# A new order of issue for the same tasks of an attention and softplus kernel

## The chip, the core and the metric

The kernel runs on one core of a Trainium2 chip. The metric is the device time of one execution in microseconds (us); lower is better. Unless another unit stands beside it, every time below is in us. The core has TensorE (PE in the profile, with its weight loads as PEld), VectorE (DVE), ScalarE (ACT), GpSimd (POOL) and SyncE (SP), which issues the DMAs here. Each engine works through its own instructions in the order in which the program issues them, and waits where an input isn't ready.

## The reference: what is computed

A long-short attention over 4 batches, 8 heads, 768 positions and 64 columns feeds a feed-forward layer with softplus (512 to 2048 to 512 columns, 3072 tokens).

```python
k_sum = k.reshape(B, H, nb, block, D).max(axis=3)      # blocks of 32 positions
v_sum = v.reshape(B, H, nb, block, D).mean(axis=3)
scores_l = scale * np.matmul(q, k.transpose(0, 1, 3, 2))
mask_l = np.abs(pos[:, None] - pos[None, :]) < window  # window 16
scores_s = scale * np.einsum('bhsd,bhnd->bhsn', q, k_sum) + np.log(block)
scores_all = np.concatenate([np.where(mask_l, scores_l, -1e9), scores_s], axis=-1)
a = softmax(scores_all)
x = np.matmul(a, np.concatenate([v, v_sum], axis=2))   # heads side by side: 3072 x 512
h = x @ w_in                                            # 512 x 2048
g = np.maximum(h, 0.0) + np.log1p(np.exp(-np.abs(h)))
out = g @ w_out                                         # 2048 x 512
```

## The kernel before

**Attention.** The work is cut into 24 units: 12 chunks of 256 tokens (three per batch), each with two halves of the heads (called 0 and 2). A unit is named by its group x, its place i in the group and its heads: a0.0.0, a0.0.2, a0.1.0 and a0.1.2 are the units of group 0, a1.0.0 and a1.0.2 those of group 1. A unit runs through scores (PE, L601), mask (DVE, L614, eight instructions, with the row's maximum), exp (ACT, L622, eight instructions, each with the read of its sum), inverse (DVE, L629 and L630), normalise (L635, on POOL or DVE), transposes, values (PE, L692), the rounded part xh (ACT, L708) and the remainder xl (DVE, L712). The four units of group 0 are transposed by PE (L648) and copied from PSUM by ACT (L652, two copies per unit, one for each half of pT). All others are transposed by DVE in squares of 32 (L661), leave by DMA to DRAM (L669) and come back in place by four DMAs (L673). Block maxima of k are taken by DVE (L329), block sums of v by POOL or DVE (L357 to L362); of the first batch they are made by PE (L407) and scaled by ACT (L420).

**Weights.** For each of the 16 slices f of 128 hidden columns a chain w0 to w15 splits the weights of both layers into a high and a low part: two loads (SP, L741 and L738), magnitude (L754 on DVE or L757 on ACT), clamp (DVE, L761), shift (DVE, L765), sign (DVE, L769), tail (L775 on ACT or L778 on DVE), add_tail (POOL, L783), high (L787, ACT or DVE) and low (L794, DVE or POOL). All of a chain but loads, magnitude and high work in a scratch tile t, of which there are two, shared with the loads of k and v for block sums and with the output tiles. w0 and w1 are made in two halves of 128x512, all others at once as 128x1024.

**Feed-forward.** Product (PE, L823) of slice f with the tokens of group x is three matmuls for each of four slices of x: high with high, high with low, low with high. ACT applies softplus twice (L843 rounded as gh, L847 exactly), DVE takes the remainder gl (L851), and PE projects gh and gl with the second weights (L860). The work of slice f in group x is named f0.6 for x = 0, f = 6. Groups 0 and 1 are run for slices 0 to 10, then for 11 to 15, with partial sums kept in DRAM (L883 to L891); the remaining groups run over all 16.

**What sets the order.** The program first declares 1593 tasks with `order.add`, each with the buffers that it reads and writes, and with one way for each engine that could run it. It then issues them one by one as a string says:

```python
        for word in sequence.split():
            task = self.tasks[int(word.rstrip("ab"))]
            assert all(other in begun for other, _ in task.after) and task not in begun
            begun.add(task)
            task.ways[" ab".index(word[-1]) if word[-1] in "ab" else 0].run()
```

A number names a task, and the letter behind it picks another way: `198` is the low part of w4 on DVE, `198a` the same on POOL; `398` is the normalise of a1.0.0 on POOL, `398a` on DVE. So the string `SEQUENCE` (L147) fixes the order on every engine, the DMA queue of SP included, and for the tasks with two ways the engine. Waits between engines follow from the buffers that the tasks share.

Of the kernel before, what the change touches and what calls it, by code (L numbers as in the profile page):

```python
# [152 lines left out]
171a 130 109 199 94 172 40 200 110 111 173 41 112 42 174 387 175 239 113 95 197 176 121 114 123 122 115 124 198
177 219 125 220 181a 178 309 209 126 182 185 318 127 201a 183 388 310 184 240 394 202 311 210 186 319 312 408
205 313 249 203 325 187 204 320 592 390 321 188 391 225 279 314 206 322 221a 315 395 316 594 250 317 207a 323
396 208 222 331 223 224 241a 326 397 324 398a 415 399 226 327 245 329 328 400 229 332 242 230 227 330 269 243
389 333 228 337 280 215 392 244 211a 334 246 335 416 338 343 212 213 339 247 214 336 248 344 345 341 417 340 216
574 401 346 393 342 595 347 591 217a 218 348 255 578 418 575 593 419 349 402 403 231a 404 289 235 232 233 355
350 234 579 236 351 352 353 576 356 290 420 357 600a 405 237a 421 270 238 603 406 358 251a 354 407 361 577a 252
580 422 253 367 362 409 254 413 412 604 256 363 425 423 359 368 411 275 424 364 410 257a 369 360 258 605 365  # L160
581a 584 414 373 588 618 259 295 606 370 366 374 585a 371 375 582 426 589 376 299 260 372 427 428 378 377 607
429 381 382a 583 383 435 300 430 431 619 432 380 436 271 437 379 438 433 272 434 273 586 441 620 274 596 617 447
442 608 276 621 443 439 448 444 609 449 265 440 450 453 277a 305 590 278a 459 454 455 456 445 587 384 446 261
451 626a 385 452 460 262 386 461 457 598 285 263 629 264 465 643 462 266 644 630 601 471 466 648a 645 467 610
458 468 472 463 267a 473 631 474 464 291 469 470 268 477 292 483 293 478 632 294 651 475 479 633a 666 484 667
485 476 281a 296 480 481 486 634 489 635 670a 282 482 297 602 498 283 612 490 284 613 665 298 491 487 499 492
286 500 652 488 301a 506 501 287a 653 302 673 288 502 794 597 303 493 797 304 494 796 507 795 512 599 495a 306
# [15 lines left out]
1056 1048 936 1049 937 938 941 942 943 1076 946 1077 1057 1058 1059 1078 1060 952 939 947 944 1079 1080a 1081
948 945 953 950 949 1082 954 1090 955 1091 1099a 951 1061 958 1062 1069 1071 1063 1083 1084 1085 1086 964 959
1070 1072 960 1074 961 1075 970 965 1093 1092 966 1094 967 1087 956 1095 1088 1097 1089 1096 1098 1102 971 1100
972 1101 957 1103 1222 962 1226 973 1104 963 968 969 974 1105 1106a 1107 975 976 1223 1108 1227 1224 1228 982
977 1109 1110 978 1111 979 980 983 1112 984 985 988 1225a 1229a 1232 994 989 990 1236 991 1239 1240 1248 1241
1000 995 1243 996 1242 1233 981 986 997 1237 1230 1006 1001 1002 1234 1238 1231 1251 987 1252 992 1003 1253 1235
993 998 999 1007 1004 1254 1255a 1256 1008 1005 1113 1009 1257 1265 1266 1274 1010 1114 1267 1011 1014 1115 1269
1268 1012 1015 1244 1013 1017 1016 1116 1018a 1258 1259 1260 1261 1019 1245 1124 1117 1247 1118 1246 1249 1119  # L190
1250 1277 1125 1126 1120 1278 1121 1122 1127 1279 1123 1128 1262 1129 1270 1271 1263 1280 1130 1273 1281a 1272
1275 1264 1276 1282 1136 1131 1283 1292 1296 1293 1132 1291 1133 1134 1137 1138 1139 1142 1284 1285 1286 1287
1148 1143 1144 1145 1288 1149 1150 1299 1294 1289 1295 1290 1135 1297 1300 1140 1298 1151 1301 1141 1146 1147
1152 1302 1303a 1153 1304 1154 1305 1314 1318 1315 1313 1160 1155 1306 1156 1307 1157 1158 1308 1161 1309 1162
1163 1166 1310 1167 1168 1321 1316 1311 1169 1317 1312 1159 1319 1322 1164 1320 1323 1165 1170 1171 1172 1324
1325a 1326 1178 1173 1327 1174 1175 1176 1179 1180 1181 1184 1328 1329 1330 1331 1190 1185 1186 1187 1196 1191
# [815 lines left out]
```

## Time and profile before

| | |
|---|---|
| median of 3 runs | 628.37 (627.63 to 628.79) |
| profiled execution | 630.34 |
| its span in the profile | 628.5 |
| mean granted clock of TensorE | 0.992 |
| PE busy | 611.5, 97% of the span |
| DVE busy | 277.5 (44%), 757 instructions |
| ACT busy | 311.7 (50%), 752 instructions |
| POOL busy | 83.2 (13%), 74 instructions |

Rows of a timeline begin with the start and the time that the row took, then engine, line, operation and tiles, the number of instructions (a row can hold several) and, in brackets, idle time before it and what ended it. Rows of groups give the number of instructions behind the shapes, then the busy time of all and the mean of one in ns. The busy share of an engine is a mean over very different stages: the weights are prepared in the first quarter of the span only, so POOL's 13% says little of that quarter.

### The profile page before, as it was taken

To read this page: it belongs to the slowest core of one execution; us is meant where nothing else is said; L and a number is where in the kernel's file an instruction comes from. 1 tells how busy PE (TensorE), PEld (TensorE's weight loads), DVE (VectorE), ACT (ScalarE), POOL (GpSimd) and SP (SyncE) were. 2 spreads that over 40 slices of the span, in tenths; PEclk is the share of its full clock that TensorE was granted. 3 is DMA by queue.
4 is the path that set the end of the run, shared out by engine and by line. 5 is a ranking of instruction groups with operands and counts; after the bars stand their busy time and mean duration, and the time that the engine had idled before them with its cause. 6 is when DMAs were issued, how large, how long until landed. Compare 5 with 4: busy or idle time off the path is not lost.

```text
span 628.5 us, 11315 instructions
## 1 busy us (share of the span) xinstructions
PE 611.5 (97%) x4348; PEld 505.5 (80%) x4348; DVE 277.5 (44%) x757; ACT 311.7 (50%) x752; POOL 83.2 (13%) x74
## 2 busy tenths in 40 slices
PE   4889999999999999999999999999999999999997
PEld 4478888888888888888888888888888888888996
DVE  5978988679644443212451444432411111341111
ACT  1789988479652554316472435462622222553222
POOL 5324341434310202101000030000000000000000
PEclk9799999999999999999999999999999999999999
DMA  8779678933767861241344553543300400311000
GB/s 292 234 244 347 217 190 242 291 92 113 231 199 212 236 181 63 86 139 43 135 152 131 176 141 107 153 144 110 100 0 1 141 0 2 108 66 68 34 1 33
DMA packets 84453, 85.72 MB, mean 136 GB/s; under 512 B 24528, under 2 KB 70192, under 8 KB 84400
## 3 DMA queue, kind: packets, MB, share of 16 engines
q1 hardware_dynamic: 84400, 85.01, 44.0%
q8 instruction: 34, 0.56, 0.4%
q14 instruction: 19, 0.16, 0.1%
HBM read 64.23 MB, written 18.35 MB: 131 GB/s over the span
## 4 chain that ended last, share of the span: by engine, by line
PE 95%; DMA 1%; issue 1%; POOL 1%; SPq 1%; ACT 0%; DVE 0%; POOLq 0%; DVEq 0%
PE po L860 42%; PE ph L823 42%; PE sc L601 4%; PE xo L692 4%; DMA first<-v_hp_dram 1%; PE vt L407 1%; PE warm L934 1%; POOL added L296 0%; SPq L555 0%; PE pt L648 0%; DVE sp L614 0%; ACT sp L622 0%; SPq L738 0%; SPq L741 0%; ACT vn L420 0%
## 5 line engine op out<-in xcount | busy, mean ns | idle before, releaser
L823 PE MATMUL ph<-xh,w 128*128 128x512 f32 (+1 forms) x896 | 257.6, 360 | 0.0
L860 PE MATMUL po<-w,gh 128*128 128x512 f32 x768 | 201.1, 392 | 0.0
L823 PEld LDWEIGHTS ph<-xh,w 128*128 128x128 f32 x896 | 161.7, 189 | 27.2 <-issue 0.5
L851 DVE TENSOR_TENSOR gl<-ph,gh 128x512 fp32r<-128x512 f32 (+1 forms) x112 | 68.1, 611 | 222.4 <-ACT ph L847 203.8
L860 PEld LDWEIGHTS po<-w,gh 128*128 128x128 f32 x768 | 142.1, 188 | 29.5 <-issue 0.5
L823 PE MATMUL ph<-xl,w 128*128 128x512 f32 (+1 forms) x448 | 160.8, 359 | 0.0
L843 ACT ACTIVATE gh<-ph 128x512 fp32r<-128x512 f32 (+1 forms) x112 | 60.2, 537 | 196.0 <-PE ph L823 169.4
L860 PE MATMUL po<-w,gl 128*128 128x512 f32 x384 | 113.7, 393 | 0.0
L823 PEld LDWEIGHTS ph<-xl,w 128*128 128x128 f32 x448 | 84.5, 189 | 13.1
L860 PEld LDWEIGHTS po<-w,gl 128*128 128x128 f32 x384 | 71.0, 188 | 15.5 <-issue 1.0
L622 ACT ACTIVATE sp<-sp,nm 128x120 f32<-128x120 f32 x192 | 73.1, 383 | 2.5 <-DVE nm L614 2.3
L847 ACT ACTIVATE ph<-ph 128x512 f32<-128x512 f32 (+1 forms) x112 | 59.4, 532 | 0.0
L783 POOL TENSOR_TENSOR t<-t,raw 128x1024 int32<-128x1024 int32 (+1 forms) x18 | 43.5, 2421 | 81.7 <-DVE t L769 24.9
L614 DVE CUSTOM_DVE_ANT_0 sp<-sc,added 128x120 f32<-128x120 f32 x192 | 40.7, 278 | 15.2 <-PE sc L601 15.0
L843 ACT ACT_TABLE_LOAD x24 | 30.8, 1283 | 33.5 <-PE ph L823 31.7
L622 ACT ACTIVATION_READ_ACCUMULATOR sp<-sp,nm 128x1 f32 x192 | 36.1, 188 | 0.0
L712 DVE TENSOR_TENSOR xl<-xo,xh 128x512 fp32r<-128x512 f32 x24 | 16.5, 687 | 39.1 <-ACT xh L708 39.1
L708 ACT CAST xh<-xo 128x512 fp32r<-128x512 f32 x24 | 14.1, 590 | 39.2 <-PE xo L692 39.2
L661 DVE STREAM_TRANSPOSE tb<-sp 128x1024 f32<-128x1024 f32 x20 | 24.8, 1240 | 2.3 <-POOL sp L635 2.0
L692 PEld LDWEIGHTS xo<-pT,v 120*64 120x64 f32 x640 | 20.3, 138 | 6.7 <-issue 6.2
L635 POOL TENSOR_TENSOR sp<-sp,ss 128x960 f32<-128x960 f32 x7 | 12.5, 1793 | 98.3 <-DVE ss L630 75.9
L622 ACT ACT_TABLE_LOAD x18 | 23.1, 1283 | 4.8 <-DVE nm L614 4.5
(64 smaller groups left out, 389.7 us busy)
## 6 DMA issues: line engine op xcount, KB each, us to landing
squares<-tb SPq DMA_DIRECT2D x20, 512.0 KB
pT<-squares SPq DMA_DIRECT2D x80, 128.0 KB
raw<-w_in_dram SPq DMA_DIRECT2D x16, 512.0 KB
raw<-w_out_dram SPq DMA_DIRECT2D x16, 512.0 KB
...
```

The lines of the kernel that those rows point to most:

```text
L601: nc.tensor.matmul(unit(g * NU + h * NPAIR + i)[r * QW:(r + 1) * QW, k0:k1], lhsT=q[rows, w * QW:(w + 1) * QW], rhs=k[rows], start=True, s ...
L614: nc.vector.tensor_tensor_reduce(out=sp()[:, n], in0=unit(n), in1=added()[:, kinds.index((lows[w], lows[w + 1]))], scale=-SCALE, scalar=FL ...
L622: nc.scalar.activation(sp()[:, n], sp()[:, n], AF.Exp, bias=nm()[:, n:n + 1], scale=-1.0, accum_out=ss()[:, n:n + 1],)
L661: nc.vector.transpose(out=tb().rearrange("p k (u q) -> p u k q", q=SQ), in_=tiles.sp().rearrange("p u (k q) -> p u k q", q=SQ),)
L692: nc.tensor.matmul(xo()[h * D:(h + 1) * D, g * CH + w * QW:g * CH + (w + 1) * QW], lhsT=tiles.v(g)[:, w, h * D:(h + 1) * D], rhs=queries(g ...
L712: nc.vector.tensor_sub(out=of_x(xl), in0=of_bank(), in1=of_x(xh).bitcast(F32))
L783: nc.gpsimd.tensor_tensor(a, a, word(0, I32), op=ALU.add)
L823: nc.tensor.matmul(ph()[:, :n_x], lhsT=w1()[:, i1, part, cc * P:(cc + 1) * P], rhs=a()[:, cc, :n_x], start=cc == 0 and i == 0, stop=cc == ...
L843: nc.scalar.activation(gh()[:, :n_x], ph()[:, :n_x], AF.Softplus)
L847: nc.scalar.activation(ph()[:, :n_x], ph()[:, :n_x], AF.Softplus)
L851: nc.vector.tensor_sub(out=gl()[:, :n_x], in0=ph()[:, :n_x], in1=gh()[:, :n_x].bitcast(F32),)
L860: nc.tensor.matmul(po[t](), lhsT=a()[:, t * P:(t + 1) * P], rhs=w2()[:, i2, part], start=f == f0 and i == 0, stop=f == f1 - 1 and i == 2,)
```

## The change

The diff replaces the text of `SEQUENCE` and nothing else. Tasks, tiles, buffers and their numbers are the same; the order differs from the first line on, and so does the choice of the engine for some tasks. The first two of its 69 lines:

```diff
 SEQUENCE = """
-2 133 43 160 45 64 68 47 1 0 96 134 3 49 4 138a 5 51 135 44 6 7 97 161a 136 8 100 137 9 142 46 10 11 165a 53 12
-162 13 163 14 72 164 55 166 57 15 73 16 17 132 139 151 50 140 84 48 74 141a 59 52 85 65 18 61 167a 189 104 143a
...
+64 43 0 2 132 44 45 68 3 4 5 47 6 49 160 51 133 53 7 8 9 10 100 96 11 12 13 14 15 16 17 18 19 151 55 59 20 46 72
+73 74 57 61 50 48 75 21 22 161a 165 23 24 1 25 26 134a 84 85 162 163 76 164 166 86 87 27 28 52 29 104 105 387
...
```

Of the tasks with two ways, the new text has the low parts of 9 weight pieces on POOL instead of 4, 13 normalises on POOL instead of 7, 6 sums of v on POOL instead of 4, and 11 magnitudes on DVE instead of 4 (7 on ACT instead of 14).

Two places show it. On POOL, from the last half-weight pieces to the normalise of a1.0.2, the order before is this; t_475 belongs to w4, the following t to w2, w3, w5, w7, w9 and w6 in this order, and the row with sp is the normalise of a1.0.2.

```order
L783 TENSOR_TENSOR t_327<-t_327,raw_160 128x512
L783 TENSOR_TENSOR t_475<-t_475,raw_292 128x1024
L783 TENSOR_TENSOR t_558<-t_558,raw_469 128x1024
L783 TENSOR_TENSOR t_648<-t_648,raw_514 128x1024
L783 TENSOR_TENSOR t_671<-t_671,raw_566 128x1024
L783 TENSOR_TENSOR t_771<-t_771,raw_628 128x1024
L783 TENSOR_TENSOR t_832<-t_832,raw_587 128x1024
L783 TENSOR_TENSOR t_928<-t_928,raw_658 128x1024
L635 TENSOR_TENSOR sp_222<-sp_222,ss_987 128x8x120
```

Now POOL has, with t_578 of w4, t_642 of w2, t_738 of w3, t_817 of w5, t_822 of w7, t_885 of w9 and t_907 of w6, and with the normalises of a0.1.2 (sp0) and a1.0.0 (sp):

```order
L635 TENSOR_TENSOR sp0_336<-sp0_336,ss_431 128x960
L783 TENSOR_TENSOR t_578<-t_578,raw_440 128x1024
L794 TENSOR_TENSOR w_639<-t_578,w_639 128x2x512
L783 TENSOR_TENSOR t_642<-t_642,raw_520 128x1024
L783 TENSOR_TENSOR t_738<-t_738,raw_523 128x1024
L794 TENSOR_TENSOR w_794<-t_738,w_794 128x2x512
L783 TENSOR_TENSOR t_817<-t_817,raw_594 128x1024
L635 TENSOR_TENSOR sp_119<-sp_119,ss_534 128x8x120
L783 TENSOR_TENSOR t_822<-t_822,raw_740 128x1024
L794 TENSOR_TENSOR w_887<-t_822,w_887 128x2x512
L783 TENSOR_TENSOR t_885<-t_885,raw_853 128x1024
L783 TENSOR_TENSOR t_907<-t_907,raw_583 128x1024
```

The weights follow one another as before; between them stand the low parts of w4, w3 and w7 and two normalises, which DVE had.

On ACT, around the first copies of pT (L652), the order before has the exponential of the last unit of group 0, the two copies of a0.0.0 with a magnitude between them, its tail, and the rounded part of the first values:

```order
L420 ACTIVATE vn0_274<-vt_276 24x512
L622 ACTIVATE sp0_344,ss_438<-sp0_344,nm_417 128x120 x8
L652 COPY pT_467<-pt_432 120x512
L757 ACTIVATE t_475<-raw_292 128x1024
L652 COPY pT_467<-pt_482 120x512
L775 ACTIVATE raw_292<-raw_292 128x1024
L708 CAST xh_522<-xo_496 128x2x256
```

Now, at the same place (sp_119 is the tile of a1.0.0, raw_361 half a weight, raw_440 w4):

```order
L622 ACTIVATE sp0_336,ss_431<-sp0_336,nm_398 128x120 x8
L420 ACTIVATE vn0_161<-vt_300 24x512
L775 ACTIVATE raw_361<-raw_361 128x512
L652 COPY pT_526<-pt_352 120x512
L622 ACTIVATE sp_119,ss_534<-sp_119,nm_496 128x120 x8
L652 COPY pT_526<-pt_529 120x512
L775 ACTIVATE raw_440<-raw_440 128x1024
L708 CAST xh_575<-xo_553 128x2x256
```

The exponential of a1.0.0, which stood behind the first softplus operations, is now between the two copies of a0.0.0.

Elsewhere in the head, POOL makes ident first, in front of the tile `added` for the masks, where it stood last of the constants. On PE, the scores of a1.0.0 and a1.0.2 stand ahead of the first product; before, they stood behind the products of f0.0 and the first half of f0.1, and among the projections of f0.1 and f0.2. On SP the loads of v for the first values stand ahead of more of the weights' loads.

More of the change, by code (lines that the diff above doesn't have):

```diff
@@ L147 @@
 SEQUENCE = """
-2 133 43 160 45 64 68 47 1 0 96 134 3 49 4 138a 5 51 135 44 6 7 97 161a 136 8 100 137 9 142 46 10 11 165a 53 12
-162 13 163 14 72 164 55 166 57 15 73 16 17 132 139 151 50 140 84 48 74 141a 59 52 85 65 18 61 167a 189 104 143a
-75 76a 147 86 54 168a 105 190 56 70 144 145 116 146 156 69 87 152a 58 101 88a 66 106 60 153 154 155 62 117 157
-19 20 63 21 148 77 71 118 22 23 24 67 107 25 108a 26 99 27 28 29 149a 103 30 150 31 32 78 169 33 158a 34 191a
-119 170 35 120a 79 102 36 80 98 37 192 195 128 81 193 179 194 89 82 129 38 90 91 159 39 180 92 83 196 131 93
@@ L153 @@
[L153 to L167, printed above, removed]
@@ L183 @@
[L183 to L196, printed above, removed]
[4 rows of a table removed]
-1375 1376 1372 1379 1377 1380 1381 1382 1378 1385 1383 1386 1387 1388 1453 1384 1467 1454 1468 1476a 1391 1470
@@ L202 @@
-1469 1455 1471 1389 1390 1392 1397 1456 1457a 1458 1393 1395 1394 1398 1459 1399 1400 1396 1403 1460 1461 1462
-1401 1404 1463 1405 1406 1402 1409 1464 1410 1411 1479 1472 1465 1412 1474 1466 1407 1473 1475 1480 1477 1408
-1478 1481 1415 1413 1416 1482 1483a 1414 1421 1484 1417 1418 1485 1419 1422 1423 1424 1420 1427 1486 1487 1488
[6 rows of a table removed]
+64 43 0 2 132 44 45 68 3 4 5 47 6 49 160 51 133 53 7 8 9 10 100 96 11 12 13 14 15 16 17 18 19 151 55 59 20 46 72
+73 74 57 61 50 48 75 21 22 161a 165 23 24 1 25 26 134a 84 85 162 163 76 164 166 86 87 27 28 52 29 104 105 387
@@ new lines @@
+135 69 167 77 168a 88 136 137 142 54 116 65 117 138 106 152 139 66 140a 56 58 60 153 107 154 62 118 189 30 190
+31 394 32 70 119 155 141a 63 71 67 108 33 34 35 156a 408 143 395 102 157 158a 144 36 37 38 147 101 145 99 103 98
+97 169 170 179 180 78 159a 79 396 128 130 146 80 39 40 41 195 42 81 89 82 129 191 192 90 209 592 131 91 193 199
+200 595 83 92 93 109 111 194 148 149 120 150 397 94 196 95 197a 198a 171 172 110 112 594 113 121 123 114 115 122
+124 175 415 125 126 388 127 173 174 181a 219 182 183 220 392 210 176 309 310 311 318 312 313 319 185 314 320 184
@@ new lines @@
+177a 178 321 322 186 187a 188a 315 316 317 323 201a 202 203 204 221 205 222 223 325 224 326 225 327 328 206 207
+208 299 239 391 240 331 332 333 398 399 334 259 226 289 229 241a 227 228a 245 215 249 300 416 242 243 244 211a
+212 246 324 329 337 213 214 330 216 338 339 340 247a 230 250 343 344 290 345 248 217a 218 335 336 341 342 417
+346 418 400 591 574 235 578 401 402 575 231 232 233 347 349 355 348 350 356 255 234 357 579 351 600 593 353 352
+419 420 403 393 390 603 236 237 238 404 389 405 576 577 354 359 358 251a 252 253 254 421 580 409 414 361 422 362
@@ new lines @@
+604 406 256 407 411 412 423 618 621 360 365 363 364 367 257a 258 366 373 605 368 369 374 375 620 584 581a 585
+424 371 606 370 607a 413 410 425 372 426 427 588 269 270 275 582 608 376 377 279 280 589 428 590 381 380 378 382
+429 430 583 379 435 271 431 432 272 273 436 437 438 274 276 260 383 433 441 447 434 439 440 442 448 443 444 295a
+453 445 446 277 278a 449 450 454 596 586 305 587 384 451 452 459 457 619 261 609 610 455 456 385 265 465 626a
+460 598 617 262 263 264 266 386 612 466 467 461 462 629 644 458 471 267 648 291 472 473 468 292 293 645 630 463
@@ new lines @@
+477 464 469 470 475 268a 474 631 602 281 632 282 476 483 643 599 651 666 597 665 613 283 294 478 601 484 670a
+479 480 481 485 284 486 489 490 491 633a 634 667 492 296 297a 635 298 498 285 286 499 482 487 488 493 494 500
+287 506 652 301 501 502 653 673 507 503 302 303 304 654 655a 656 288a 794 802 795 495 496 508 512 513 514 509
+515 504 505 657 796 797 306 518 519 520 307a 308 524 674 675 521 676 497 611 793 845 614 622 625 532 636 805 624
+638 510 511 516 639 627 846 615 525 616 526 527 623 677 678 806 807 628 637 820 821 823 517 522 523 640 641 819
@@ new lines @@
+530 540 822 541 528 531 679 542 808 642 536 646 809 543 810 647 658 659 660 546 547 529 548 828a 552 534 661 650
+549 533 831 553 554 555 832 833 834 649 662 663 537 664 544 545 558 559 535 811 550 668 669 551 556 680 672 682
+683 564 557 560 561 565 538 862 562 671 681 863 570 866 563 864 835 566 567 684 798 569 568 685 686 687 836 803
+812 814 804 695 837 688 689 800 571 690 539 865 691 692 693 572 815 573 701 849 813 696 697 698 850 702 871a 703
+707 694 708 709 704 699 853 801 799 816 838 874 817 710 888 875 818 854 889 857 891 839 858 700 713 705 706 892
@@ new lines @@
+847 719 711 712 714 851 876 897a 890 900 824 826 720 721 715 848a 877 716 852a 878 879 717 718 1021 1025a 855
+723 725 856 722 901 880 726 724 727 728 729 825 827 859 1022 830 840 902 829 1020 903 731 732 733 1028 841 842
+843 734 844 881 1043 1222 867 884 1044 730 735 860 861 736 1047a 882 883 1230 737 743 904 872 905 1029 1030 738
+739 1031 740 1032a 906 744 745 741 742 868 1042 873 869 746 749 1050 870 885 886 750 907 893 894 896 747 748 753
+898 909 1223 1231 1065 1033 899 1066 751 895 1051 752 1064 1068 910 1052 887 755 908 1067 756 757 758 761 754
@@ new lines @@
+1053 1054a 1073a 1076 1034 911 1035 1234 1023 1091 1027 1094 1038 1037 1024 762 763 764 759 760 767 1055 1099a
+1077 1078 912 765 1079 1080a 913 768 769 766 773 1056 1092 771 1224 770 772 779 774 1026 775 1093 1090 1102 1081
+776 1235 1036 1039 777 1228 780 781 778 1103 782 783 914 1225 1104 1040 1041 1082 1239 915 1240 1241 1057 1242
+1060 916 917 1229 785 922 928 1105 923 924 784 1226 1045 1046 1227 925 1106 787a 1049 1048 786 918 1059 1243
+790a 791a 929 1058 788a 1107 930 1108 1061 1248a 1251 1266 1069 1070 1268 1062 1072 1267 931 1063 1083 1274 919
@@ new lines @@
+920 921 926 934 935 940 1075 941 1085 1252 927 932 1265 1074 933 938 936 937 939 1253 942 943 944 1086 1084 1269
+1277 1071 1292 1087 946 1088 947 1109 1293 789 948 1089 945 1232 1296 949 1291 1254 1255a 1256 1278 1279 952 950
+951 953 958 1299 959 956 1280 1281a 954 955 960 1257 1282 1300 1314 1112 964 965 966 1095 1100 1110 961 967 1301
+957 962 1111 1318a 963 968 969 1313 1315 1096 1101 1097 792 1098 1113 1258 1283 1244 1321 1441 1246 1114 1259
+1261 1260 970 1442 1236 1443 1247 1115 1302 1450a 976 971 1245 972 973 977 978 974 975 982 983 1303a 979 984
@@ new lines @@
+1304 1322 988 989 990 985 991 980 994 1000 995 996 981 997 1233 1237a 986 1001 1238 1249 1250 987 1002 1003 992
+1006 1007 1262 993 998 999 1444 1270 1275 1284 1285 1008 1009 1263 1264 1004 1323 1005 1276 1010 1012 1011 1013
+1014a 1116 1124 1117 1118 1119 1017 1120 1018a 1015a 1121 1125 1126 1122 1127 1272 1271 1445 1123 1453 1287 1286
+1273 1288 1289 1290 1305 1294 1128 1130 1131 1132 1136 1129 1133 1134 1135 1142 1137 1140 1138 1143 1139 1141
+1324 1325a 1144 1145 1326 1295 1306 1148 1454 1154 1309 1308 1455 1297 1149 1150 1151 1155 1307 1146 1147 1327
@@ new lines @@
+1156 1152 1153 1158 1298 1160 1161 1157 1310 1311 1328 1316 1162 1159 1164 1163 1165 1312 1166 1167 1456 1168
+1169 1172 1178 1457a 1458 1173 1174 1175 1184 1179 1170 1468 1330 1470 1331 1171 1185 1186 1176 1177 1182 1180
+1459 1329 1019 1320 1181 1190 1183 1188 1191 1192 1187 1189 1193 1196 1197 1319 1317 1332 1446 1198 1194 1195
+1451 1452 1199 1333 1334 1447 1200 1201 1202 1208 1203 1467 1204 1209 1210 1205 1211 1471 1016 1449 1335 1336
+1337 1338 1460 1206 1207 1212 1216 1215 1343 1213 1217a 1218 1344 1345 1339 1214 1340 1349 1350 1351 1219a 1341
@@ new lines @@
+1461 1462 1469 1220a 1346 1448 1355 1342 1463 1356 1352 1357 1358 1361 1347 1348 1362 1353 1354 1464 1476a 1479
[4 rows of a table added]
+1490 1426 1431 1491 1492 1432 1493 1499 1494 1495 1435 1496 1500 1436a 1434 1433 1501 1502 1497 1498 1505 1503
+1506 1507 1504 1511 1508 1512 1513 1509 1514 1438a 1517 1518 1523 1510 1515 1516 1524 1519 1520 1529 1521 1525
+1526 1522 1535 1527 1528 1530 1531 1532 1536 1537 1541 1542 1439a 1543 1538 1544 1533 1534 1539 1547 1548 1540
+1545 1546 1553 1549 1551 1437 1440 1554 1555 1550 1556 1559 1565 1560 1561 1562 1566 1567 1552 1568 1571 1557
@@ L211 @@
+1572 1573 1558 1574 1563 1564 1577 1578 1579 1580 1583 1569 1570 1575 1576 1581 1582 1584 1585 1586 1587 1589
+1591 1588 1590 1592
 """
```

5 lines of the change are left out of this document (removed), and 24 rows, old and new, of the table SEQUENCE.

## The prediction

> **What bounds the kernel now.** I read the page's slices and chain first, then the busy time by stretches.
>
> ```profile
> span 628.5 us, 11315 instructions
> PE   4889999999999999999999999999999999999997
> PE 95%; DMA 1%; issue 1%; POOL 1%; SPq 1%; ACT 0%; DVE 0%; POOLq 0%; DVEq 0%
> ...
> 40.00:49.60 9.60, 6.84 (x87) 5.85 (x86) 5.62 (x7) 6.89 (x10) 4.17 (x2) 0.82 0.98 291
> 49.60:85.60 36.00, 36.00 (x277) 29.48 (x274) 32.83 (x70) 35.43 (x66) 14.85 (x6) 1.00 0.76 259
> 44.90:48.30 3.40, 3.40 (x38) 2.94 (x37) 2.75 (x4) 2.95 (x4) 2.11 (x1) 0.50 0.88 287
> ```
>
> The columns of a stretch are its length, then PE, PEld, DVE, ACT, POOL, then the granted clock. TensorE is on 95% of the chain and is never idle in 49.60–85.60; only the head has holes. The set of products is the same in both kernels, so the time moves only if the first product (T1 below, 49.60 in before) moves, if TensorE work crosses T1, or if TensorE has to wait afterwards. DVE at 32.83 and ACT at 35.43 of 36.00 say that a wait is near. DVE and POOL look slack together only until single instructions are read:
>
> ```profile
> 18.77 1.28 POOL L794 TENSOR_TENSOR w<-t,w 128x512 fp32r<-128x512 f32 x1 [1.87 <-DVE w L787]
> 19.05 2.00 DVE L635 TENSOR_TENSOR sp<-sp,ss 128x960 f32<-128x960 f32 x1
> 25.86 1.16 DVE L635 TENSOR_TENSOR sp<-sp,ss 128x960 f32<-128x960 f32 x1
> 28.46 0.28 DVE L614 CUSTOM_DVE_ANT_0 sp<-sc,added 128x120 f32<-128x120 f32 x1
> 28.77 2.52 POOL L783 TENSOR_TENSOR t<-t,raw 128x512 int32<-128x512 int32 x2 [8.73 <-DVE nm L614]
> 30.08 1.24 DVE L629 TENSOR_SCALAR ss<-ss 128x8 f32<-128x8 f32 x1
> 51.06 0.69 DVE L761 TENSOR_SCALAR t<-t 128x1024 f32<-128x1024 f32 x1
> 67.29 1.16 DVE L635 TENSOR_TENSOR sp<-sp,ss 128x960 f32<-128x960 f32 x1
> 67.48 3.26 POOL L783 TENSOR_TENSOR t<-t,raw 128x1024 int32<-128x1024 int32 x1 [5.13 <-DVE ss L630]
> 74.51 2.44 POOL L783 TENSOR_TENSOR t<-t,raw 128x1024 int32<-128x1024 int32 x1 [3.77 <-DMA raw<-w_in_dram]
> 76.42 1.07 DVE L761 TENSOR_SCALAR t<-t 128x1024 f32<-128x1024 f32 x1
> ```
>
> The normalise L635 takes 1.16, but 2.00 when it starts inside a POOL operation: that one ends at 20.05, and 1.00 of work follows. The clamp L761 takes 0.69, but 1.07 at 76.42, ending 0.54 after POOL. L629 takes 1.24 at 30.08 behind POOL's pair. The other way round, POOL's L783 takes 2.44 alone and 3.26 when L635 began first. The mask L614 (28.46 to 30.08, 1.62 for a unit) ran inside POOL's 28.77–31.29 unharmed. So a set of DVE operations and POOL's take turns on one thing; I call it the port. The groups between the end of w4's low part (49.7) and of w6's (84.9):
>
> ```profile
> L794 DVE TENSOR_TENSOR w<-t,w 128x1024 fp32r<-128x1024 f32 x6 | 7.3, 1222 | 0.3 <-ACT w L787 0.2
> L769 DVE SCALAR_TENSOR_TENSOR t<-raw,t 128x1024 uint32<-128x1024 uint32 x5 | 6.1, 1224 | 0.1
> L761 DVE TENSOR_SCALAR t<-t 128x1024 f32<-128x1024 f32 x5 | 4.2, 840 | 0.0
> L765 DVE TENSOR_SCALAR t<-t 128x1024 uint32<-128x1024 uint32 x5 | 3.9, 772 | 0.1
> L787 DVE CAST w<-t 128x1024 fp32r<-128x1024 f32 x2 | 1.4, 694 | 1.2 <-POOL t L783 1.1
> L630 DVE RECIPROCAL ss<-ss 128x8 f32<-128x8 f32 x1 | 0.2, 203 | 0.0
> L629 DVE TENSOR_SCALAR ss<-ss 128x8 f32<-128x8 f32 x1 | 0.2, 165 | 0.0
> L783 POOL TENSOR_TENSOR t<-t,raw 128x1024 int32<-128x1024 int32 x5 | 14.8, 2961 | 19.5 <-DMA raw<-w_out_dram 7.9 <-DVE ss L630 5.1 <-DMA raw<-w_in_dram 3.8
> ...
> 83.68 1.23 DVE L794 TENSOR_TENSOR w<-t,w 128x1024 fp32r<-128x1024 f32 x1
> 84.67 1.07 PE L860 MATMUL po<-w,gl 128*128 128x512 f32 x4
> 85.57 0.39 PE L823 MATMUL ph<-xh,w 128*128 128x512 f32 x1
> ```
>
> With undisturbed durations: DVE 6×1.22 + 5×1.22 + 10×0.69 + 2×0.69 + 0.37 + 1.16 = 23.2, POOL 5×2.44 = 12.2; together 35.4 of port in 35.2 us. The port is full, and w6's low part, done at 84.91, is only 0.66 ahead of f0.6 at 85.57. **Port work ahead of a weight is therefore time, with almost no slack.**
>
> **The change, part by part.** First the head, whose rows are these.
>
> ```profile
> 31.39 0.40 ACT L622 ACTIVATE sp<-sp,nm 128x120 f32<-128x120 f32 x1
> ...
> 34.34 0.19 ACT L622 ACTIVATION_READ_ACCUMULATOR sp<-sp,nm 128x1 f32 x1
> 34.55 0.59 ACT L652 COPY pT<-pt 120x512 f32<-120x512 f32 x1
> ...
> 35.98 1.43 PE L692 MATMUL xo<-pT,first 120*64 120x64 f32 x32
> 44.36 2.06 PE L692 MATMUL xo<-pT,first 120*64 120x64 f32 x32 [2.66 <-ACT pT L652]
> 49.60 0.50 PE L823 MATMUL ph<-xh,w 128*128 128x512 f32 x1
> ```
>
> *Earlier exponentials, but one more ahead of the first values.* An exponential of a unit takes 3.1 (31.39 to 34.53), and in before the fourth ends at 34.5. With ident first on POOL and scores and masks drawn forward, I lay the new rows out with the same durations and get 30.2 (29.5–30.9). But ACT now has the exponential of a1.0.0 between the two copies of the first unit's pT. It waits for its mask, which on DVE stands behind an inverse (0.4), a sign, a tail and a magnitude of half a weight (half of 1.22 + 0.69 + 0.69, so 1.3) and the mask itself (1.6): 30.2 + 3.3 = 33.5, end of the exponential 36.6, copy 37.2 at best. POOL now also has a normalise (1.79) and half an L783 and half an L794 (1.28 each, by the row of 18.77) there; taking turns, that is up to 4.3 later. So the first values move from 35.98 to 37.2–41.5, and I take 40.5, three quarters of the way, since each of the three was seen to block above. From first values to T1 it was 13.6, of which 2.66 was the idle seen at 44.36 (v's DMA behind a weight's, which the new SP order undoes). With the score task now inside (1.3), and up to 1.3 for half clock after an idle (44.90–48.30: 0.50), it is 10.9–13.5; I take 12.9. T1 = 53.4 (48.1–55.0): **+3.8** (−1.5 to +5.4).
>
> *Scores ahead of T1.*
>
> ```profile
> 53.90 0.41 PE L601 MATMUL sc<-kf,q 64*64 64x96 f32 x8
> ...
> 55.22 0.50 PE L823 MATMUL ph<-xh,w 128*128 128x512 f32 x1
> ...
> 67.80 0.42 PE L601 MATMUL sc<-kf,q 64*64 64x96 f32 x8
> ...
> 69.12 1.19 PE L860 MATMUL po<-w,gh 128*128 128x512 f32 x4
> ```
>
> Two score tasks of 1.32 leave the stretch after T1: **−2.6**.
>
> *Port work ahead of w6.*
>
> ```profile
> L635 POOL TENSOR_TENSOR sp<-sp,ss 128x960 f32<-128x960 f32 x7 | 12.5, 1793 | 98.3 <-DVE ss L630 75.9 <-DMA v<-v_hp_dram 22.4
> ...
> L794 POOL TENSOR_TENSOR w<-t,w 128x1024 fp32r<-128x1024 f32 x2 | 5.0, 2490 | 2.4 <-DVE vs L369 1.3 <-ACT w L787 1.2
> ```
>
> f0.6 is 35.97 after T1 in before; less the two scores (2.64) and less four products of f0.5 moved behind it (0.90, from 84.67 to 85.57), it comes due at T1+32.4. In the new order DVE reaches w2's shift only behind the last xl, about T1+1.5, where before had w2 finished (51.1). From there to w6's low part the order lists: DVE 6 shifts, 5 clamps, 4 high copies and 1 magnitude (16×0.69 = 11.0), 6 signs and 4 lows (10×1.22 = 12.2); POOL 6 L783 (14.6), two lows of weights, w3 and w7, which before had on DVE at 1.22 and which now take 2.4–2.5 each (4.9), and one normalise (1.8). Sum 44.5. With the port always busy w6 is ready at T1+46; with the holes that the chain of each weight leaves, T1+48.7. The same walk gives w2 T1+13.5 (due 10.3), w3 T1+18, w5 T1+31 (due 22.5). The waits add up to w6's lateness: 46…48.7 − 32.4 = 13.6–16.3; since starts lie some 0.08 closer than durations, 12.6 is the floor. I take **+14.5**. Behind w6 the order has 19 of port up to w10, due 22 after f0.6, so nothing more there; w13 may be late by 0–6, nearest to 0.
>
> *The clock.* An idle of 2.66 at 44.36 was followed by 3.4 at clock 0.50, costing 1.7. Waits of 3–8 invite the same; those before the last are hidden in the next wait. **+1.3**.
>
> *Rest.* The DMAs are the same ones on the same queue. Behind the weights the port has only normalises and sums of v left, of which more stand on POOL now (1.79 instead of 1.16); TensorE's products lie beside them, and I cost that at nothing. Were that cover gone, each late unit would add about its exponential, 3, and an upper bound is one such unit for w13's phase, inside the 0–6.
>
> The page "SBUF — State Buffer" of the Trainium skill, section "Who interferes with whom", says that a VectorE operation in a two-port mode, or one with two SBUF inputs against a GpSimd operation that reads SBUF, shares a lock with GpSimd, held for a whole instruction. L635 agrees: 2.00 against 1.16. It speaks for counting L769, which no row here shows blocked, giving the 44.5; without L769, L754 and L787 it would be 33.7.
>
> Sum: +3.8 − 2.6 + 14.5 + 1.3 = **+17.0**. The profiled execution took 630.34 (1.84 around its span), 1.97 above the median of 628.37; 647.3 by it, so **645.4** against the median.
>
> **The rivals.**
> 1. *Only the kinds that a row shows blocked take turns* (L629, L635, L761, L765, L794 with POOL). For: L769, L787 and L754 never overlap POOL in the rows quoted. Against: 35.4 in 35.2 needs them. Port work is then 44.5 − 6×1.22 − 5×0.69 = 33.7, w6 at T1+36.9 with holes, 4.5 late; T1 +2.5; −2.6; clock +0.7: **633.5**.
> 2. *The port doesn't bind the new order; it is faster.* DVE alone, with five L851 (0.68), a transpose (1.25) and a mask, needs 29.5: w6 at T1+31, ready before T1+32.4, no wait at all. T1 at 50.8 at worst: 628.4 + 1.2 − 2.6 = 627.0; with T1 unmoved **625.7**. It decides at w6's readiness, T1+32.4. Against it speak all pairs quoted above.
> 3. *The order doesn't act as listed*, since other waits end last and hide both sums: about 628.4. Little speaks for it: TensorE was never idle, so any late weight shows.
>
> **How the numbers follow.** The full exclusion has 0.70, the first rival 0.15, the second 0.08, the third 0.07. The forecast's own range is 637–655 (−1.5 or +5.4 for T1, 12.6–16.3 for the waits, 0–6 at w13, not all at once). With the first rival the range is 630–655; it leaves out the rivals below and a tail above, some 0.2. A measurement here can tell about 0.2%, 1.26 us, from no change: faster 0.07, same 0.08, slower 0.85.
>
> **What would show it.** In the stretch after T1, TensorE idle for 13–16 in pieces, each ended by ACT or DVE at f0.2, f0.3, f0.5 and f0.6; many DVE clamps and signs stretched by POOL; w6's low part on DVE ending 46–49 after T1; T1 at 51–55 with the second copy of the first pT behind an exponential. I am wrong if L769 runs 1.22 inside a POOL operation, if w6 is ready by T1+37, or if TensorE idles at the ends of groups instead.

## The result, and the profile after

| | before | after |
|---|---|---|
| median | 628.11 (627.63 to 628.79, 4 runs) | 653.89 (652.99 to 655.44, 4 runs) |
| ratio | | 1.0412, 95% interval 1.0387 to 1.0437 |
| profiled execution | 630.34 | 653.18 |
| its span | 628.5 | 651.4 |

The new order is slower by 25.8 us in the medians and by 22.9 in the spans of the two profiled executions, which are taken apart below. From the page of after, its engines, the slices of TensorE and the chain that ended last:

```profile
span 651.4 us, 11283 instructions
...
PE 620.0 (95%) x4348; PEld 509.6 (78%) x4348; DVE 304.2 (47%) x743; ACT 298.5 (46%) x742; POOL 116.2 (18%) x96
...
PE   7888789998999999999999999999999999999997
...
PE 65%; DVE 12%; ACT 8%; DMA 7%; issue 4%; SPq 3%; POOL 2%; POOLq 0%; ACTq 0%; DVEq 0%
```

TensorE's share of the chain fell from 95% to 65%, and what came in its place is DVE, ACT and DMA. Its busy time grew by 8.5, about 4.8 of it by half clock (19.4 of TensorE's busy time lie in stretches of clock 0.50, and 9.8 in before), and its idle time by 14.4. Two stretches follow, from the end of w4's low part to that of w6's and from w10's to w15's, first of before and then of after (start and end, length, then PE, PEld, DVE, ACT, POOL busy, then the clock, the DMA share and GB/s):

```profile
49.70:84.90 35.20, 35.20 (x270) 28.80 (x271) 32.18 (x66) 34.63 (x66) 14.81 (x5) 1.00 0.76 259
104.60:163.50 58.90, 58.90 (x429) 50.62 (x429) 45.49 (x104) 41.62 (x101) 23.38 (x12) 1.00 0.57 174
```

```profile
48.60:96.40 47.80, 37.35 (x135) 27.91 (x135) 45.99 (x52) 31.27 (x47) 22.45 (x10) 0.89 0.52 183
117.40:182.80 65.40, 62.25 (x431) 51.79 (x430) 53.76 (x96) 38.29 (x95) 27.48 (x16) 0.97 0.52 160
```

From w4 to w6 it takes 47.8 instead of 35.2, and DVE is busy for 46.0 of them. What DVE does there is seen in its costliest groups, of after, with two of POOL's:

```profile
L761 DVE TENSOR_SCALAR t<-t 128x1024 f32<-128x1024 f32 x6 | 10.5, 1755 | 1.4 <-ACT t L757 1.3
L765 DVE TENSOR_SCALAR t<-t 128x1024 uint32<-128x1024 uint32 x6 | 9.8, 1641 | 0.2
L794 DVE TENSOR_TENSOR w<-t,w 128x1024 fp32r<-128x1024 f32 x4 | 9.0, 2241 | 0.1
L769 DVE SCALAR_TENSOR_TENSOR t<-raw,t 128x1024 uint32<-128x1024 uint32 x6 | 7.3, 1222 | 0.2
L787 DVE CAST w<-t 128x1024 fp32r<-128x1024 f32 x4 | 4.7, 1184 | 0.0
...
L783 POOL TENSOR_TENSOR t<-t,raw 128x1024 int32<-128x1024 int32 x6 | 15.4, 2570 | 16.0 <-DVE t L769 11.5 <-DMA raw<-w_in_dram 2.5 <-issue 2.0
L794 POOL TENSOR_TENSOR w<-t,w 128x1024 fp32r<-128x1024 f32 x2 | 4.8, 2410 | 5.6 <-ACT w L787 3.3 <-DVE w L787 2.4
```

The clamp's mean is 1.76 us against 0.69 alone, the shift's 1.64 against 0.69, the low part's 2.24 against 1.22, the high copy's 1.18 against 0.69. Over the 20 operations that is 18.2 us of DVE's time; the same reckoning gives 1.2 for the groups of before that the prediction shows. Single rows of DVE and POOL show why, and settle which kinds wait:

```profile
45.84 2.78 POOL L794 TENSOR_TENSOR w<-t,w 128x1024 fp32r<-128x1024 f32 x1 [1.51 <-DVE w L787]
46.40 2.77 DVE L761 TENSOR_SCALAR t<-t 128x1024 f32<-128x1024 f32 x1
...
90.27 2.42 POOL L783 TENSOR_TENSOR t<-t,raw 128x1024 int32<-128x1024 int32 x1 [2.04 <-DVE t L769]
90.56 2.69 DVE L787 CAST w<-t 128x1024 fp32r<-128x1024 f32 x1
...
158.74 2.41 POOL L783 TENSOR_TENSOR t<-t,raw 128x1024 int32<-128x1024 int32 x1 [6.86 <-DVE t L769]
158.91 3.32 DVE L769 SCALAR_TENSOR_TENSOR t<-raw,t 128x1024 uint32<-128x1024 uint32 x1
```

A sign L769 of 1.22 takes 3.32 and a high copy L787 of 0.69 takes 2.69 behind one POOL instruction; they end 1.08 and 0.56 after POOL does, a little less than one own duration. So the kinds that the rows of before didn't show take turns with POOL too.

TensorE's waits in after up to the second stretch of weights, and the low part ahead of f0.6:

```profile
46.39 0.50 PE L823 MATMUL ph<-xh,w 128*128 128x512 f32 x1
50.42 0.50 PE L823 MATMUL ph<-xl,w 128*128 128x512 f32 x1 [2.14 <-DVE xl L712]
...
75.14 0.79 PE L823 MATMUL ph<-xh,w 128*128 128x512 f32 x1 [4.71 <-DVE gl L851]
90.70 1.19 PE L860 MATMUL po<-w,gl 128*128 128x512 f32 x4 [2.62 <-DVE gl L851]
95.17 0.59 PE L823 MATMUL ph<-xh,w 128*128 128x512 f32 x1
...
162.62 0.50 PE L823 MATMUL ph<-xh,w 128*128 128x512 f32 x1 [1.88 <-DVE gl L851]
187.03 1.15 PE L692 MATMUL xo<-pT,v 120*64 120x64 f32 x32 [0.90 <-DMA pT<-squares]
...
95.15 1.22 DVE L794 TENSOR_TENSOR w<-t,w 128x1024 fp32r<-128x1024 f32 x1
```

The first product starts at 46.39, 3.2 earlier than in before. Much of that may be chance. The run further down that keeps the order and engines of before up to 128 us starts it at 46.91 and not at 49.60, and the one that keeps those of after at 46.74:

```profile
46.91 0.50 PE L823 MATMUL ph<-xh,w 128*128 128x512 f32 x1
...
46.74 0.50 PE L823 MATMUL ph<-xh,w 128*128 128x512 f32 x1
```

What comes behind it repeats well: w6 is ready 35.3 behind the first product in before and in that run, and 50.0 behind it in after and in the other.

The profile puts several waits down to DVE's gl, since the remainder stands in DVE's queue behind blocked weight work. f0.6 begins at 95.17 instead of 85.57, while w6's low part is still being made (from 95.15 on; the first matmuls need the high part only).

For the runs below I add up, from the single rows, the time in which the port is in use: some POOL addition, subtraction or multiplication, or some DVE operation of the kinds that take turns with it (those of the weights, L635, L629, the block sums of v and the copy L508), stands in the trace (overlaps count once). Mask, transposes, block maxima, gl and xl are not among these kinds: of gl and xl of 128x512, 84 and 32 in the 13 traces start inside a POOL operation of 0.9 us or more with at least 0.5 us of it left, and none takes over 0.70. One of them, in after:

```profile
112.68 2.43 POOL L783 TENSOR_TENSOR t<-t,raw 128x1024 int32<-128x1024 int32 x1 [1.22 <-issue]
114.24 0.69 DVE L712 TENSOR_TENSOR xl<-xo,xh 128x512 fp32r<-128x512 f32 x1
```

The rest is the port's idle time. Counted from 4.5 us, in which before begins with its first weight, a low part's end is 4.5 + busy + idle. That holds by construction: the table divides a time, and what caused it is for the runs to show.

| busy + idle | to w4 | w4 to w6 | w6 to w10 | w10 to w15 | w6 ready | time |
|---|---|---|---|---|---|---|
| before | 33.1 + 12.1 | 33.6 + 1.6 | 17.3 + 2.4 | 47.6 + 11.3 | 84.9 | 628.1 |
| after | 31.9 + 12.2 | 42.6 + 5.2 | 17.6 + 3.4 | 50.3 + 15.1 | 96.4 | 653.9 |
| old order, new engines | 38.0 + 9.3 | 38.0 + 2.8 | 17.7 + 3.8 | 50.1 + 14.3 | 92.6 | 645.2 |
| before + POOL work | 33.1 + 11.5 | 39.2 + 1.3 | 18.0 + 1.9 | 47.6 + 10.8 | 89.5 | 634.7 |
| after, short lows on POOL | 27.5 + 11.9 | 39.0 + 6.6 | 17.6 + 3.4 | 45.6 + 17.7 | 89.6 | 645.2 |
| new order, old engines | 27.1 + 18.1 | 38.2 + 14.2 | 17.1 + 5.2 | 47.8 + 26.6 | 102.1 | 675.1 |
| new head, old rest, old engines | 27.2 + 19.1 | 38.2 + 9.0 | 17.3 + 3.2 | 47.6 + 11.3 | 97.9 | 643.9 |
| after, DVE behind its producer | 29.5 + 14.5 | 39.8 + 6.8 | 18.0 + 3.3 | 48.7 + 18.2 | 95.1 | 653.5 |
| old head, new rest | 32.9 + 10.7 | 37.8 + 14.4 | 17.6 + 3.5 | 50.7 + 14.9 | 100.3 | 658.1 |
| new head, old rest | 32.2 + 11.2 | 38.1 + 2.4 | 17.3 + 4.0 | 47.6 + 11.3 | 88.4 | 635.9 |
| new until f1.0, then old | 31.9 + 12.6 | 42.5 + 5.2 | 17.6 + 3.4 | 48.0 + 11.2 | 96.7 | 644.2 |
| old until f1.0, then new | 32.9 + 9.6 | 33.7 + 1.4 | 17.2 + 3.1 | 49.8 + 17.5 | 82.2 | 639.7 |
| exponential behind the copy | 31.9 + 12.1 | 42.6 + 5.2 | 18.0 + 3.4 | 50.7 + 14.3 | 96.3 | 654.9 |

Up to w6 after has 7.8 more of busy port than before and 3.7 more of idle port; up to w15 it has 10.8 and 8.5 more, and w15 comes at 182.8 instead of 163.5. So the port's work is two thirds of the delay at w6 and little more than half of it at w15; the table doesn't tell what makes the idle part.

### The profile page after: what moved, and what is told of

Its sections match the earlier page's. It is cut to its first block, busy times and chain, and to the rows that moved or that the text cites. A ratio compares the mean times of both kernels' runs of the same rounds, so it can differ in the third digit from the quotient of the medians.

```text
span 651.4 us, 11283 instructions
## 1 busy us (share of the span) xinstructions
PE 620.0 (95%) x4348; PEld 509.6 (78%) x4348; DVE 304.2 (47%) x743; ACT 298.5 (46%) x742; POOL 116.2 (18%) x96
## 4 chain that ended last, share of the span: by engine, by line
PE 65%; DVE 12%; ACT 8%; DMA 7%; issue 4%; SPq 3%; POOL 2%; POOLq 0%; ACTq 0%; DVEq 0%
PE po L860 31%; PE ph L823 29%; ACT sp L622 3%; PE xo L692 3%; DVE t L761 2%; PE sc L601 2%; DVE t L765 2%; DVE t L769 2%; DMA raw<-w_in_dram 1%; DMA pT<-squares 1%; DMA kf<-kT_dram 1%; ACT L843 1%; ACT gh L843 1%; DVE gl L851 1%; DMA raw<-w_out_dram 1%
## 5 line engine op out<-in xcount | busy, mean ns | idle before, releaser
L823 PE MATMUL ph<-xh,w 128*128 128x512 f32 (+1 forms) x896 | 261.3, 364 | 8.7 <-DVE gl L851 7.4
L860 PE MATMUL po<-w,gh 128*128 128x512 f32 x768 | 203.8, 395 | 1.7 <-ACT gh L843 1.6
L823 PEld LDWEIGHTS ph<-xh,w 128*128 128x128 f32 x896 | 163.6, 191 | 39.4 <-DVE gl L851 9.2
L823 PE MATMUL ph<-xl,w 128*128 128x512 f32 (+1 forms) x448 | 162.8, 363 | 2.1 <-DVE xl L712 2.1
L823 PEld LDWEIGHTS ph<-xl,w 128*128 128x128 f32 x448 | 85.6, 191 | 16.2 <-DVE xl L712 2.6
L635 POOL TENSOR_TENSOR sp<-sp,ss 128x960 f32<-128x960 f32 x13 | 24.4, 1873 | 284.0 <-DVE ss L630 210.8
L783 POOL TENSOR_TENSOR t<-t,raw 128x1024 int32<-128x1024 int32 (+1 forms) x18 | 41.4, 2300 | 49.7 <-DVE t L769 32.1
L843 ACT ACT_TABLE_LOAD x22 | 28.2, 1283 | 17.0 <-PE ph L823 14.9
L357 POOL TENSOR_TENSOR st<-st 96x512 f32<-96x512 f32 (+1 forms) x16 | 18.5, 1156 | 95.8 <-DVE gl L851 43.4
```

The costliest lines, as they stand in the source:

```text
L357: engine.tensor_tensor(rows[:, :n], rows[:, :n], rows[:, n:2 * n], op=ALU.add)
L635: engine.tensor_tensor(sp(), sp(), s, op=ALU.mult)
L783: nc.gpsimd.tensor_tensor(a, a, word(0, I32), op=ALU.add)
L823: nc.tensor.matmul(ph()[:, :n_x], lhsT=w1()[:, i1, part, cc * P:(cc + 1) * P], rhs=a()[:, cc, :n_x], start=cc == 0 and i == 0, stop=cc == ...
L843: nc.scalar.activation(gh()[:, :n_x], ph()[:, :n_x], AF.Softplus)
L860: nc.tensor.matmul(po[t](), lhsT=a()[:, t * P:(t + 1) * P], rhs=w2()[:, i2, part], start=f == f0 and i == 0, stop=f == f1 - 1 and i == 2,)
```

## The experiments

Theory 1 is the prediction's: DVE and POOL take turns, so the work on both ahead of a weight sets when it is ready. Theory 2 puts the cost on the order alone: what stands ahead of what in each queue. All kernels but two differ from before and after in `SEQUENCE` only; behind the stretch in which they differ the tasks are the same.

**The new engines in the old order.** The order of before; 74 tasks take the way that after gives them. A piece of it:

```diff
-121 114 123 122 115 124 198 177 219 125 220 181a 178 309
+121 114 123 122 115 124 198a 177a 219 125 220 181a 178 309
```

> The order of before, but each task on the engine that it has in after. Up to w6's low part 11.1 us more work on the port than before, up to w10's 12.5, up to w15's 16.1. Theory 1 (port): w6 ready at 94 to 97 us, w10 at 115 to 118, time 640 to 650. Theory 2 (order): 627 to 632.

Measured: 645.16 in its one execution, w6 at 92.6, w10 at 114.1; the port is busy for 9.3 more than in before up to w6 and 12.2 more up to w15. Order unchanged, engines changed: 17.3 us over its before (627.89, no execution above 629.0). That is theory 1's result, with w6 1.4 earlier than it said.

**More work for POOL alone.** Before, with operations whose result nobody reads:

```diff
...
                 nc.gpsimd.tensor_tensor(a, a, word(0, I32), op=ALU.add)
+                if f in (3, 5, 7, 9, 6):
+                    for _ in range(5):
+                        nc.gpsimd.tensor_tensor(extra(), ident(), ident(), op=ALU.add)
...
```

> Before, with 25 further additions of a 128x128 constant on POOL (5 each behind the tail of w3, w5, w7, w9 and w6) that nothing waits for; at about 0.45 us each 11.3 us more on POOL, which is busy for 14.9 of the 36 us there. Port theory: DVE's weight operations wait for them, w6 ready at 93 to 96 instead of 84.9, time 635 to 641. If POOL is only a slack engine: time 628 to 629, w6 at 85 to 86.

Measured: 634.65 in its one execution, 6.8 over its before, w6 at 89.5: not a slack engine, though the time falls just short of theory 1's range and w6 came 3.5 earlier than it said. The group of these 25:

```profile
L787 POOL TENSOR_TENSOR extra<-ident 128x128 f32<-128x128 f32 x25 | 19.2, 768 | 1.6
```

Alone (beside the mask, say) one takes 0.40; the mean is 0.77, so they wait for DVE as DVE waits for them. The 23 ahead of w6's end are 9.2 us of work, and from w4 to w6 it took 40.5 instead of 35.2, 5.3 more. Six of the 23 ran at 0.40 beside DVE operations that take no turns (gl, mask, transpose), and a low part beside one of the others took 1.30 to 1.42 instead of 1.22.

**Less work for POOL, nothing moved.** In after, low parts on POOL are made for 64 of 512 columns only; the products use the high part in such a low part's place, so that TensorE has the same work and the output lacks terms:

```diff
...
-                engine.tensor_tensor(part(1, F32R), rows(t), part(0, F32), op=ALU.subtract)
...
+                c = DM
+                if engine is nc.gpsimd:
+                    c = 64
+                    short.update(keys)
+                engine.tensor_tensor(
+                    part(1, F32R)[:, :, :c], rows(t)[:, :, :c], part(0, F32)[:, :, :c], op=ALU.subtract,
+                )
...
```

> After, with every instruction in its place, but the low parts of weights that stand on POOL computed for 64 of 512 columns only (products with these weights use the high part in the low part's place, so the output lacks those terms; TensorE has the same work). At 0.4 instead of 2.4 us, and 0.3 instead of 1.3 for half weights, the port has some 9 us less up to w6 and 13 less up to w15, and no task changes its engine or place. Port theory: w6 ready at 87 to 91 instead of 96.4, time 639 to 647. If the queues' order or the chains of the weights hold it, with POOL as a slack engine: w6 at 94 to 97, time 651 to 655.

Measured: 645.18, w6 at 89.6. The port's busy time up to w6 fell by 8.0 and w6 came 6.8 earlier; the time fell by 8.7. Every queue is as in after, so this part of the loss is POOL's time and not the order. That it acts by way of the port is seen on DVE: up to w6 its operations take some 7 us less beyond their own durations than in after.

**The old engines in the new order.** A piece of the text of after, and of the kernel run:

```diff
-387 135 69 167 77 168a 88 136 137 142 54 116 65 117
+387 135 69 167a 77 168a 88a 136 137 142 54 116 65 117
```

> The order of after, but each task on the engine that it has in before. Durations summed from the rows give 11.1 us less work on the port of DVE and POOL up to w6's low part than after, 12.5 less up to w10's (as much as before in both), 16.0 less up to w15's. Theory 1 (the port sets when weights are ready, and the engines chosen cost the time): w6 ready at 84 to 87 us, w10 at 104 to 107, time 627 to 634. Theory 2 (the order itself costs it: what stands ahead of what on each engine): 648 to 655, with w6 at 94 to 97. Something halfway says that both do.

Measured: 675.12 (ratio to before 1.0768, 1.0732 to 1.0804), the slowest of all, and outside what either theory said; the first product comes at 55.6. The busy time up to w6 fell to 65.3, just below the 66.7 of before, as reckoned, but the port stood idle for 32.3 us instead of 17.4 in after and 13.7 in before.

**The head alone, with the old engines.** The string of after up to the first product, then the remaining tasks in the order of before, all with the engines of before; the seam, in after and in this kernel:

```diff
-392 210 176 309 310 311 318 312 313 319 185
+392 210 176 239 177 178 309 185 318 201a 310 184 240 202
```

> The order of after up to the first product, then the order of before, each task on the engine that it has in before. The first product comes 2 to 4 us earlier than in before and the two scores stand ahead of it. Port theory: the port work ahead of w6 is that of before, so w6 is ready at 83 to 87 and the gain in front of it is lost in waits: 625 to 630. If the first product set the time: 628.1 - 3.2 - 2.6 = 622.3.

Measured: 643.87 (1.0254, 1.0233 to 1.0274), far above what either theory said; first product at 57.7, w6 at 97.9. The first product isn't earlier but 8 later. Rows of DVE, of ACT, and TensorE's wait:

```profile
41.38 0.69 DVE L761 TENSOR_SCALAR t<-t 128x1024 f32<-128x1024 f32 x1 [3.38 <-ACT t L757]
...
44.79 3.36 DVE L635 TENSOR_TENSOR sp<-sp,ss 128x960 f32<-128x960 f32 x1
...
47.16 1.04 ACT L787 CAST w<-t 128x1024 fp32r<-128x1024 f32 x1 [3.04 <-POOL t L783]
48.78 1.13 ACT L757 ACTIVATE t<-raw 128x1024 f32<-128x1024 f32 x1 [0.58 <-DMA k<-kT_dram]
49.81 1.06 ACT L652 COPY pT<-pt 120x512 f32<-120x512 f32 x2
...
50.44 1.98 PE L692 MATMUL xo<-pT,first 120*64 120x64 f32 x32 [5.94 <-ACT pT L652]
```

The normalise of the fourth unit, whose inverse was there at 32.4, stands in DVE's queue at POOL's place: behind w4's clamp, which waits 3.38 for a magnitude on ACT. On ACT the copies of the third unit's pT stand behind w4's high copy, which after has on DVE and which waits 3.04 for POOL, and behind w2's magnitude; TensorE waits 5.94 for them. So this run and the one before don't test the order of after by itself: a place in the string that costs nothing on one engine is a wait in another engine's queue.

**The moved tasks back on DVE, each behind what feeds it.** 14 tasks (8 normalises, 6 low parts; the expectation counts 13), for instance:

```diff
-66 140a 56 58 60 153 107 154 62 118 189 30 190 31
+66 140a 56 58 60 153 107 108a 154 62 118 189 30 190 31
```

> The order of after, with the 13 normalises and weights' low parts that went from DVE to POOL back on DVE, each directly behind the task that feeds it (the inverse, or the high copy) rather than where POOL had it. Port work up to w6's low part 7.4 us less than after, up to w15's 9.7 less. If port work is what costs, and the bad result of the order with the old engines came from DVE tasks standing in the queue where they were laid out for POOL: w6 ready at 87 to 91 us, w15 at 171 to 176, time 641 to 648. If the new order needs these tasks on POOL: 654 or more, with port idle up to w6 well above the 12.3 us of after.

Measured: 653.48, w6 at 95.1, w15 at 183.4. Here the forecast fell. The port's busy time went down by 5.2 up to w6 and 6.4 up to w15, less than the 7.4 and 9.7 reckoned, and its idle time went up by 3.9 and 7.0. What is taken from POOL lengthens DVE's queue, in which the mask, gl and xl stand too. I take this to be why the two nearly cancel, but no run shows it. Which of the added waits it is, one by one, I haven't followed.

**Which stretch.** Four kernels join the two strings, with the engines of the part that a task comes from. First the seam at the first product, in after and in the kernel that joins new head and old rest:

```diff
-210 176 309 310 311 318 312 313 319 185
+392 210 176 239 177 178 309 185 318 201a 310 184 240 202
```

> The order and engines of after up to the first product, those of before behind it. Port work up to w6 6.0 us above before, up to w10 5.9, up to w15 6.0; first product 3 us earlier than in before and two scores ahead of it. Port theory: w6 ready at 89 to 93, w10 at 109 to 113, time 633 to 639. If the stretch behind the first product is what costs: 622 to 626.

Measured: 635.88 (1.0106, 1.0063 to 1.0149), w6 at 88.4, w10 at 109.7, first product at 45.7: the time as forecast, with w6 0.6 earlier than said. The earlier first product is worth nothing here, since w2, w3 and w6 come late behind it (w6 42.7 behind it, in before 35.3).

> The order and engines of before up to the first product, those of after behind it. Port work up to w6 4.5 us above before, up to w10 5.8, up to w15 9.7. Port theory: first product at 49 to 50, w6 ready at 88.5 to 91, w15 at 172 to 175, time 636 to 642. If the head of the new order is what costs: 628 to 631.

Measured: 658.07 (1.0459, 1.0417 to 1.0500), far off, w6 at 100.3. The reason is at the seam:

```profile
49.72 0.42 PE L601 MATMUL sc<-kf,q 64*64 64x96 f32 x8 [1.72 <-DMA q<-qT_dram]
54.58 0.62 PE L601 MATMUL sc<-kf,q 64*64 64x96 f32 x8 [3.48 <-DMA q<-qT_dram]
```

The two scores come ahead of the first product, as in after, but their queries are loaded late, as in before, so TensorE, and with it everything behind, waits (first product at 56.9, port idle for 14.4 between w4 and w6). It says nothing of after.

Then the seam at the first product of group 1, new before old and old before new; the seam of the first of them, against after:

```diff
-428 590 381 380 378 382 429 430 583 379 435 271 431 432
+381 380 378 382 295 260 429 583 383 435 430 431 619 432
```

> The order and engines of after up to the first product of group 1 (128 us), those of before behind it. In the profiles the port needed 58.9 us from w10's to w15's low part in before and 65.4 in after, and TensorE lost another 3.6 behind w15 in after, in waits for attention units. If the second stretch of the new order costs these two: 641 to 646, w15 some 59 us behind w10. If the whole loss is made in the first 128 us: 652 to 655.

> The mirror: order and engines of before up to the first product of group 1, those of after behind it. By the same two terms 6.5 + 3.6 us above before: 635 to 641, w15 64 to 67 us behind w10. If the whole loss is made in the first stretch: 627 to 630. A wait of its own where the two orders meet can add to either.

Measured: 644.17 (1.0252, 1.0206 to 1.0297) and 639.74 (1.0181, 1.0137 to 1.0225). With the old second stretch, w15 comes 59.2 behind w10, as in before, and the time is 9.7 below after; with the new one, it comes 67.3 behind w10 and the time is 11.8 above before. Both times agree with the two terms given ahead. So of the 25.8, some 16 are lost in the first 128 us and some 10 to 12 in what follows; 16.2 and 11.8 over before make 28.0, 2.2 more than the whole.

**The exponential between the copies.**

```diff
-159a 79 396 128 130 146 80 39 40 41
+159a 79 128 130 146 80 396 39 40 41
```

> After, with the exponential of a1.0.0 on ACT behind both copies of the first unit's pT instead of between them. The copy that came at 34.15 us can come at about 29, so the values of the first unit lose their wait of 2.4. Port theory: the weights set the time behind the head, w6 ready at 94 to 98, time 651 to 656 whatever the first values gain. If the place of the exponential costs the time: first product 1.5 to 3 earlier and time 650 to 652 with w6 at 92 to 94.

Measured: 654.85, w6 at 96.3, first product at 47.05 (46.39 in after). The wait of 2.44 in the first values is gone and comes back as one of 2.93 in front of the second values; nothing else moves. What the prediction took for a cost of the head is none that shows here.

## Why the prediction was right, and where it wasn't

The direction, the cause and the place were right; the time came out 8.5 above the forecast of 645.4, inside the range. That it is so near is in part luck: two terms were mis-sized with opposite signs, the head by 7.0 too late and what follows w6 by 11.4 too little. With the head as measured the forecast would have been 638.4, 15.5 too low.

1. *What bounds: the port, full from w4 to w6, with w6 just ahead of f0.6.* Right, though it is not all of the loss. In before the port is in use for 33.6 of 35.2 there; the 35.4 of the forecast is a sum of single durations, and starts lie closer. Adding work on POOL alone, taking some away alone, and changing only the engines all moved w6 and the time in the direction of the port's work; the last two nearly by its amount, the short additions by little more than half of theirs. But 3.7 of the 11.5 by which w6 is later stand in the table as idle port, and the forecast's slack of 0.66 was read too small, since f0.6 begins before the low part is done.
2. *All kinds of the weights' chain take turns.* Right, against rival 1: L769, L787 and L754 are seen blocked in after (an L754 of 0.69 takes 1.20 at 98.58 and 1.42 at 140.59). What the Trainium skill's "SBUF — State Buffer", section "Who interferes with whom", says of VectorE operations with two SBUF inputs holds for L769 here: 3.32 instead of 1.22.
3. *The walk through the weights behind the first product.* Right: w2 at T1 + 13.5, w3 + 18, w5 + 31, w6 + 46 to 48.7 were forecast; measured from 46.39 they are + 15.0, + 18.7, + 31.8 and + 50.0, the last a little beyond what was said. TensorE's lateness against an undisturbed run of the new order is 17.3 at f0.7, half clock included (0.90 granted in that stretch); forecast were 14.5 + 1.3. The parts are not as forecast: TensorE stands idle for 10.8 and not for 13 to 16, and most of the rest goes in three stretches of 3.4 at clock 0.50, each of which costs up to 1.7.
4. *The head: T1 at 53.4, +3.8.* Wrong: 46.39, −3.2, outside the term's own range, as are the two joined runs with the head and engines of after (46.74 and 45.67). The −3.2 itself is uncertain, since the head of before gave 46.91, 48.96 (in the run with POOL work) and 49.60. ACT's rows show the two errors. The exponentials of group 0 were through at 26.8, not at 30.2, and the exponential of a1.0.0 did not wait for the whole mask: it started at 31.10, in the midst of a mask that ran from 30.72 to 32.42, since each of its eight instructions needs one of the mask's. The second copy came at 34.15, not at 37 to 41:

```profile
26.62 0.19 ACT L622 ACTIVATION_READ_ACCUMULATOR sp<-sp,nm 128x1 f32 x1
...
28.16 0.58 ACT L652 COPY pT<-pt 120x512 f32<-120x512 f32 x1
31.10 0.39 ACT L622 ACTIVATE sp<-sp,nm 128x120 f32<-128x120 f32 x1 [2.36 <-DVE nm L614]
...
34.15 0.56 ACT L652 COPY pT<-pt 120x512 f32<-120x512 f32 x1
```

5. *Two scores ahead of T1: −2.6.* Right as a shift (they end at 45.1), though worth nothing while weights are late.
6. *Nothing behind w6 (0, at most 6 at w13).* Too small. TensorE lost another 11.4 behind f0.7: 7.2 up to w15, for which the forecast summed the port's work only as far as w10 (behind it the new order has 2.7 more busy and 3.8 more idle port), and 4.3 later, part of it in waits for attention units, such as 0.90 for pT's DMA at 187.03. The two runs joined at f1.0 confirm the size, 9.7 and 11.8, both of them with what follows w15.

The sum in spans: −3.2 − 2.6 + 17.3 + 11.4 = 22.9. Forecast were +3.8 − 2.6 + 15.8 + 0. The medians differ by 3 more, because the profiled execution of before lay 2.2 above its median and that of after 0.7 below; the late first product of before may be a part of these 2.2.

What stays open: why the new order, given back its old engines, is so much worse (+21 over after) beyond the waits shown in the head, which waits ate the gain of the run with tasks back on DVE, and what makes the port's idle time in after. No run here is faster than before. TensorE never idles in before from 49.60 on, so a gain in the order would have to come from the head, with the weights ready as much earlier, and no run that computes the whole result had that.
